# A masked-attention and MLP kernel: additive masks and zero products for the first batch, and a new place in the load order for half a weight

## The chip, the cores and the metric

The kernel runs on one core of a Trainium2 chip. The metric is the device time of one execution in microseconds (us). A quoted time is the median of several executions. A program on one core has no second die to compare with, so an execution is called slow when it lies over 1.5% above the fastest one of the same kernel; ratios use the fast executions alone. The engines are called TensorE (PE in the profile, PEld for its weight loads), VectorE (DVE), ScalarE (ACT), GpSimd (POOL) and SyncE (SP).

## The reference

Attention over 8 batches, 8 heads, 576 positions and 64 columns, followed by a two-layer MLP with the Mish activation over the 8 x 576 = 4608 rows:

```python
rel = pos[:, None] - pos[None, :]
mask_local   = (rel >= 0) & (rel < 32)                                # heads 0 to 3
mask_strided = (rel >= 0) & (pos[None, :] % 32 == pos[:, None] % 32)  # heads 4 to 7
scores = np.where(mask, q @ k.T / sqrt(64), -1e9)
x = (softmax(scores) @ v).transpose(0, 2, 1, 3).reshape(4608, 512)
h = x @ w_in                      # 512 x 2048
out = (h * tanh(softplus(h))) @ w_out   # 2048 x 512
```

Inputs and output are fp32; the kernel computes in bf16 with fp32 sums.

## The kernel before

The MLP goes in nine blocks of 512 rows. Attention of batch 0 runs ahead of it, attention of batch t+1 is woven between the second-layer products of block t. Loads on SyncE's DMA queue bring fp32 that an engine casts; loads on GpSimd's DMA queue cast on the way. From batch 2 on, q and k are turned by DMA transposes, on SyncE's queue too. "Local" tiles end in `l`, strided ones in `s`. These are the parts that the change and the argument touch:

```python
def load_qk_str(b):              # strided k, q: cast on the way, GpSimd's queue
    for dst, src in ((ks, k), (qs, q)):
        nc.gpsimd.dma_start(dst[b % 2][0:PN], src[b, 4:8]...)
def load_qk_loc(b): ...          # local k, q as fp32: SyncE's queue
def load_v(b): load_v_str(b); load_v_loc(b)      # fp32: SyncE's queue
def load_w_in(f0, f1): ...       # GpSimd's queue
def load_w_out(c0, c1): ...      # GpSimd's queue, four pieces in all
def transpose_loc(b):            # kTl, qTl, kTl, qTl: DMA transposes
    for hp in range(2):
        for src, dst in ((kl, kTl[:, hp, 32:]), (ql, qTl[:, hp, :])):
            nc.sync.dma_start_transpose(dst..., src[b % 2]...)
...
def mask(self, kind, i, meng):   # multiply exp(scores) by a mask of 0 and 1
    meng.tensor_tensor(out=pm, in0=pm, in1=mk..., op=ALU.mult)
...
a = Attn(0)
for hp in range(2):              # fp32 strided k, then q: cast, transpose
    cast(Dv, ks[0][0:PN, h:h + 2, :], st0[0][:, h:h + 2, :])
    t_step(0, "s", "k", hp, Sc)
...
for x in (ks, qs):
    Po.memset(x[1][64:SU], 0.0)
Po.tensor_copy(held[:], vs[0][0:1, 3, 0, 0:4])   # GpSimd waits, then loads w_in
load_w_in(0, 256)
... # the other four pieces of w_in, a third of v's cast, local attention
load_qk_str(1)
load_w_out(0, 2)
nc.sync.dma_start(gate[:], w_in[0:1, 0, 1536:1792])  # SyncE waits for w_in
load_v(1)
gT, g1 = mlp1(0, accs)
...
load_qk_loc(2)

def rest_of_w_out():
    Po.tensor_copy(held[:], kTl[0:1, 1, 32:36])      # GpSimd waits for kTl of batch 1
    load_w_out(2, 4)
    load_qk_str(2)
    cast_qk_loc(2, Po, Po)
...
        elif i == 2 and t + 1 < B:                   # block t, third group
            if t + 2 < B:
                load_v(t + 2)
            for b in range(max(3, t + 2 + (t > 1)), min(t + 4, B)):
                load_qk_str(b)                       # t == 1: batches 3 and 4
```

A one-row copy to `held` or a small DMA to `gate` is how the kernel makes an engine's queue wait for data before its next loads.

The softmax here doesn't subtract the row's maximum and nothing guards it: scores larger than these inputs give would overflow.

## Time and profile before

| | before |
|---|---|
| time, three executions | 320.9 us (319.92 to 322.61) |
| span of the profiled one | 319.1 us |
| TensorE busy | 300.1 us, 94% |
| VectorE / ScalarE / GpSimd busy | 127.9 / 172.6 / 41.4 us |
| bytes moved by DMA | 46.72 MB |
| mean granted TensorE clock | 0.999 |

A busy share is an average over the run. Here TensorE is full from the third block on, so what counts is its waits in the first 85 us and what ended each of them. The prediction below shows these views.

### The profile page before, as it was taken

The numbers are of one execution on the slowest core, as the hardware profiler recorded it, in microseconds if no ns is written. First come the engines' busy times: TensorE is split into PE (matmuls) and PEld (weight loads), VectorE is DVE, ScalarE is ACT, GpSimd is POOL, SyncE is SP. The second block draws the span as 40 slices with busy tenths as digits, with TensorE's granted clock in tenths as the row PEclk, the third lists the DMA queues.
The fourth block names the chain that finished last, engine by engine and source line by source line (L and its number), as shares of the span: only waits on it lengthen the run. The fifth ranks groups of instructions, "written<-read, shape, count | busy, mean of one in ns | idle before, by whom it ended". The sixth has DMA issues, their size and how long they took to land.

```text
span 319.1 us, 5867 instructions
## 1 busy us (share of the span) xinstructions
PE 300.1 (94%) x2488; PEld 159.3 (50%) x2488; DVE 127.9 (40%) x332; ACT 172.6 (54%) x195; POOL 41.4 (13%) x50
## 2 busy tenths in 40 slices
PE   0678999999899999999999999999999999999995
PEld 0564455544454445444578555445544554444444
DVE  7672168600577047703870388028802820000000
ACT  2574563476437573767375746664666466315601
POOL 9288030145000100200020000000000000000000
PEclk9999999999999999999999999999999999999999
DMA  6999999999999999999979995898340100011011
GB/s 172 213 235 206 220 212 191 177 221 212 181 184 211 175 192 221 179 153 178 211 160 165 188 208 109 155 191 144 109 83 0 68 32 36 0 66 66 2 59 73
DMA packets 103114, 46.72 MB, mean 146 GB/s; under 512 B 85168, under 2 KB 95728, under 8 KB 103088
## 3 DMA queue, kind: packets, MB, share of 16 engines
q1 hardware_dynamic: 91648, 37.22, 64.6%
q0 software_dynamic: 11152, 8.92, 18.6%
q8 instruction: 19, 0.31, 0.4%
q10 hardware_dynamic: 288, 0.21, 0.2%
q14 instruction: 7, 0.06, 0.1%
HBM read 38.34 MB, written 9.44 MB: 150 GB/s over the span
## 4 chain that ended last, share of the span: by engine, by line
PE 81%; DVE 11%; DMA 4%; ACT 1%; issue 1%; SPq 0%; ACTq 0%
PE psh L428 38%; PE pso L467 28%; PE po L305 4%; PE pso L449 4%; DMA qTl<-ql 3%; PE ps L278 3%; DVE x_l L317 3%; DVE x_s L317 2%; PE trx L344 2%; DVE Pl L289 1%; DVE ks L151 1%; DVE rden L316 1%; DMA st<-in_k_dram 1%; PE trx L354 1%; PE tr L207 1%
## 5 line engine op out<-in xcount | busy, mean ns | idle before, releaser
L428 PE MATMUL psh<-xT,w_in 128*128 128x512 bf16 (+1 forms) x640 | 127.3, 360 | 0.0
L467 PE MATMUL pso<-w_out,gT 128*128 128x512 bf16 x512 | 126.3, 379 | 0.0
L433 ACT ACTIVATE gT<-psh 128x1024 bf16<-128x1024 f32 x72 | 73.6, 1023 | 44.0 <-PE psh L428 43.4
L428 PEld LDWEIGHTS <-w_in 128*128 128x128 bf16 x640 | 62.7, 98 | 62.2 <-issue 1.3
L467 PEld LDWEIGHTS <-gT 128*128 128x128 bf16 x512 | 43.6, 97 | 39.0
L289 DVE TENSOR_TENSOR Ps<-Ps,consts_sb 72x864 bf16<-72x864 bf16 (+1 forms) x24 | 13.2, 551 | 88.8 <-ACT Ps L283 88.8
L149 ACT COPY xT<-trx 128x576 bf16<-128x576 bf16 x32 | 20.1, 639 | 37.7 <-PE trx L354 28.2
L474 ACT COPY osb<-pso 128x1024 f32<-128x1024 f32 x16 | 16.2, 1012 | 22.6 <-PE pso L467 13.8
L283 ACT ACTIVATE Ps<-ps 72x864 bf16<-72x864 f32 (+1 forms) x24 | 18.5, 803 | 14.8 <-PE ps L278 14.8
L316 DVE RECIPROCAL rden<-po 72x4 f32<-72x4 f32 (+1 forms) x100 | 17.4, 174 | 18.8 <-PE po L305 18.6
L317 DVE TENSOR_TENSOR x_s<-po,rden 72x256 bf16<-72x256 f32 x56 | 23.5, 420 | 1.9
L151 DVE COPY osb<-pso 128x512 f32<-128x512 f32 (+1 forms) x2 | 1.1, 558 | 54.5 <-PE pso L449 54.5
L283 ACT ACTIVATE Pl<-ps 128x960 bf16<-128x960 f32 (+1 forms) x24 | 18.7, 806 | 3.6 <-PE ps L278 3.5
L305 PEld LDWEIGHTS <-Ps 72*128 72x128 bf16 x256 | 13.9, 101 | 12.5 <-DVE Ps L289 2.3
L317 DVE TENSOR_TENSOR x_l<-po,rden 96x256 bf16<-96x256 f32 x44 | 18.5, 420 | 1.5
L305 PE MATMUL po<-vs,Ps 72*128 72x65 bf16 x256 | 17.6, 201 | 0.9 <-DVE x_s L331 0.5
L97 POOL DMA_DIRECT2D ks<-in_k_dram x7 | 5.9, 842 | 80.7 <-DMA kTs<-ks 80.7
L305 PE MATMUL po<-vl,Pl 128*128 128x65 bf16 x192 | 12.9, 201 | 2.2 <-DVE x_s L317 0.7
L449 PE MATMUL pso<-w_out,gT 128*128 128x512 bf16 (+1 forms) x80 | 14.0, 336 | 0.0
L305 PEld LDWEIGHTS <-Pl 128*128 128x128 bf16 x192 | 9.9, 103 | 6.4 <-DVE x_l L317 1.8
L289 DVE TENSOR_TENSOR Pl<-Pl,consts_sb 128x960 bf16<-128x960 bf16 (+1 forms) x24 | 13.1, 545 | 0.0
L151 DVE CAST vl<-vl 128x768 bf16<-128x768 f32 x12 | 10.9, 942 | 0.8 <-DMA vl<-in_v_dram 0.8
(70 smaller groups left out, 178.0 us busy)
## 6 DMA issues: line engine op xcount, KB each, us to landing
out_dram<-osb SPq DMA_DIRECT2D x16, 512.0 KB, 3.6
vl<-in_v_dram SPq DMA_DIRECT2D x7, 768.0 KB
vs<-in_v_dram SPq DMA_DIRECT2D x8, 576.0 KB
kl<-in_k_dram SPq DMA_DIRECT2D x7, 576.0 KB, 8.7
ql<-in_q_dram SPq DMA_DIRECT2D x7, 576.0 KB, 9.4
w_out<-in_moe_w_out_dram POOLq DMA_DIRECT2D x4, 512.0 KB, 15.2
ks<-in_k_dram POOLq DMA_DIRECT2D x7, 288.0 KB, 8.0
qs<-in_q_dram POOLq DMA_DIRECT2D x7, 288.0 KB, 9.4
```

Of the source, the lines that this page charges most:

```text
L149: nc.scalar.copy(out_, in_)
L151: eng.tensor_copy(out_, in_)
L283: nc.scalar.activation(pt[0:n, :, 0:nw], ps[0:n, :, o0:o0 + nw], AF.Exp, scale=scale)
L289: meng.tensor_tensor(out=pm, in0=pm, in1=mk[0:n, :].unsqueeze(1).unsqueeze(1).to_broadcast([n, 2, nu, w]), op=ALU.mult,)
L305: nc.tensor.matmul(po[:, h, :], lhsT=pt[0:n, c0:c0 + 128], rhs=rhs, start=True, stop=True,)
L316: nc.vector.reciprocal(rden[0:m, :], po[0:m, :, D])
L317: nc.vector.tensor_tensor(out=dst.rearrange("p (h d) -> p h d", h=4), in0=po[0:m, :, 0:D], in1=rden[0:m, :].unsqueeze(2).to_broadcast([m, ...
L428: nc.tensor.matmul(ps[:, u, o:o + n], lhsT=w_in[:, cc, fc * 128:(fc + 1) * 128], rhs=xT[:, cc, a:a + n], start=(cc == 2), stop=(cc == 1),)
L433: nc.scalar.activation(gT[:, 2 * g:2 * g + 2, :], ps[:], AF.Mish)
L449: nc.tensor.matmul(p, lhsT=gT[:, fc, 128 * ot:128 * ot + 128], rhs=w_out[:, fc, c0:c1], start=(fc == 0), stop=(fc == 15),)
L467: nc.tensor.matmul(p[:, ot % 2, :], lhsT=gT[:, fc, 128 * ot:128 * ot + 128], rhs=w_out[:, fc, :], start=(fc == 0), stop=(fc == 15),)
L474: nc.scalar.copy(osb[:], p[:])
```

## The change

The intent is to begin the MLP earlier and to bring the loads in the order of need. A load whose issue is made to wait for another load's data is called held below; the small DMA that does this on SyncE's queue is the gate. Batch 0's masks become products with a large negative bias that start the score sums; 64 products of zeros keep TensorE busy while it waits; GpSimd's memsets are moved and halved; local v of batch 0 is cast in three pieces on three engines; w_out's second half is issued only when local v of batch 1 has landed; the loads of local q and k of batch 2 come after w_out's third piece; and local v of batch 1 is cast on GpSimd. The first piece of w_in now waits for local q of batch 0 instead of the cast of strided v. The cut leaves out a new layout of local q and k of batch 0 (64 rows of nine positions instead of 96 of six) and a new order of batch 0's products and copies.

```diff
+    zero = const.tile([128, 128], BF16, name="zero")
+    def clear(eng, x):
+        eng.memset(x.bitcast(F32), 0.0)
+    def busy(n, i_acc):
+        ps = acc(i_acc, "ps")
+        for _ in range(n):
+            nc.tensor.matmul(ps[:, 0, 0:128], lhsT=zero[:], rhs=zero[:], start=True, stop=True)
+        def bias(self, kind, i, i_acc):    # ident x bias mask into the score sums
 ...
         a = Attn(0)
+        busy(40, 0)
 ...                                        # 8 + 8 more, and 4 + 4 in xt
+        sb = [a.bias("s", i, i) for i in (1, 2)]
-        a.mask("s", 0, Dv)                 # all six masks of batch 0 go
 ...
-        for x in (ks, qs):
-            Po.memset(x[1][64:SU], 0.0)
-        Po.tensor_copy(held[:], vs[0][0:1, 3, 0, 0:4])
+        Po.tensor_copy(held[P0:P0 + 1], ql0[0:1, 3, 0, 0:4])
         load_w_in(0, 256)
+        for x in (ks, qs):
+            clear(Po, x[1][64:SU].rearrange("p h x -> p (h x)"))
 ...
-        cast_v_loc(0, Po, 0, 3)            # and (0, Sc, 3, 6)
+        cast_v_loc(0, Po, 0, 2)            # and (0, Sc, 2, 4), (0, Dv, 4, 6)
 ...
-        load_qk_loc(2)
         def rest_of_w_out():
-            Po.tensor_copy(held[:], kTl[0:1, 1, 32:36])
+            Po.tensor_copy(held[0:1], vl32[0:1, 3, NW - 1, 0:4])
             load_w_out(2, 4)
             load_qk_str(2)
+            cast_v_loc(1, Po)
+            nc.sync.dma_start(gate[:], w_out[0:1, 8, 0:256])
+            load_qk_loc(2)
             cast_qk_loc(2, Po, Po)
 ...
-                at[6].append(lambda: cast_v_loc(1, Dv, 0, 3))
-                at[7].append(lambda: cast_v_loc(1, Dv, 3, 6))
```

Below, "the front" means all of this but the last two hunks, and "the order" means w_out behind v and q, k of batch 2 behind w_out. The cast of v of batch 1 on GpSimd belongs to neither.

More of the change, by code (lines that the diff above doesn't have):

```diff
@@ L21 @@
 CS, PN = 8, 72
+C0, P0 = 9, 64
 RING = 4
@@ L30, in _consts @@
     p = np.arange(PN)
-    c = np.zeros((128, 128 + WQ + PN), np.float32)
+    c = np.zeros((128, 128 + 2 * WQ + 2 * PN), np.float32)
     c[:, 0:128] = np.eye(128)
     c[:, 128:128 + WQ] = (rel >= 0) & (rel < STRIDE)
-    c[:PN, 128 + WQ:] = (p[:, None] % 4 == p[None, :] % 4) & (p[:, None] <= p[None, :])
+    o = 128 + WQ + PN
+    c[:PN, 128 + WQ:o] = (p[:, None] % 4 == p[None, :] % 4) & (p[:, None] <= p[None, :])
+    c[:, o:o + WQ] = -30000.0 * (1 - c[:, 128:128 + WQ])
+    c[:PN, o + WQ:] = -30000.0 * (1 - c[:PN, 128 + WQ:o])
     return c.astype(ml_dtypes.bfloat16)
@@ L54 @@
     xT = const.tile([128, 4, RT], BF16, name="xT")
-    consts = const.tile([128, 128 + WQ + PN], BF16, name="consts_sb")
+    consts = const.tile([128, 128 + 2 * WQ + 2 * PN], BF16, name="consts_sb")
     ident = consts[:, 0:128]
@@ L58 @@
     stm = consts[0:PN, 128 + WQ:128 + WQ + PN]
+    locb = consts[:, 128 + WQ + PN:128 + 2 * WQ + PN]
+    stmb = consts[0:PN, 128 + 2 * WQ + PN:]
+    zero = const.tile([128, 128], BF16, name="zero")
     vl32 = const.tile([128, 4, NW, D], F32, name="vl32")
@@ L75 @@
     gate = const.tile([1, 256], BF16, name="gate")
-    held = const.tile([1, 4], BF16, name="held")
+    held = const.tile([128, 4], BF16, name="held")
     x_l = const.tile([128, NW, 256], BF16, name="x_l")
@@ L189, in cast_v_loc @@
     def cast_v_loc(b, eng, i0=0, i1=NW):
-        for i in range(i0, i1, 3):
+        n = 3 if i1 - i0 > 2 else 2
+        for i in range(i0, i1, n):
             cast(
-                eng, vl[b % 2][:, i:i + 3, :, 0:D],
-                vl32[:, :, i:i + 3, :].rearrange("p h w d -> p w h d"),
+                eng, vl[b % 2][:, i:i + n, :, 0:D],
+                vl32[:, :, i:i + n, :].rearrange("p h w d -> p w h d"),
             )
@@ L233, in t_step_loc0 @@
         tr = tile_t("tr")[:].bitcast(BF16)
-        for j in range(CL):
+        for j in range(C0):
             for e in range(2):
                 nc.tensor.transpose(
-                    tr[64 * e:64 * e + 64, PL * j:PL * j + PL], src[0:PL, 2 * hp + e, j, :],
-                    ident[0:PL, 0:PL],
+                    tr[64 * e:64 * e + 64, P0 * j:P0 * j + P0], src[:, 2 * hp + e, j, :],
+                    ident[P0:128, P0:128],
                 )
         cast(
-            eng, dst.rearrange("c (p j) -> c p j", j=CL),
-            tr[:, 0:S].rearrange("c (j p) -> c p j", j=CL),
-        )
+            eng, dst.rearrange("c (p j) -> c p j", j=C0),
+            tr[:, 0:S].rearrange("c (j p) -> c p j", j=C0),
+        )
+    def busy(n, i_acc):
+        ps = acc(i_acc, "ps")
+        for _ in range(n):
+            nc.tensor.matmul(ps[:, 0, 0:128], lhsT=zero[:], rhs=zero[:], start=True, stop=True)
     T_ORDER = [(kd, w, hp) for kd in ("s", "l") for hp in range(2) for w in ("k", "q")]
@@ L261, in __init__, with qk @@
             self.b = b
-        def qk(self, parts, i_acc):
-            ps, o = acc(i_acc, "ps"), 0
+        def bias(self, kind, i, i_acc):
+            n, w, mk = (128, WQ, locb) if kind == "l" else (PN, PN, stmb)
+            nu = len(PARTS[kind][i])
+            ps = acc(i_acc, "ps")
+            for e in range(2):
+                nc.tensor.matmul(
+                    ps[:, e, 0:nu * w].rearrange("p (u c) -> p u c", u=nu), lhsT=ident[0:n, :],
+                    rhs=mk.unsqueeze(1).to_broadcast([n, nu, w]), start=True, stop=True,
+                )
+            return ps
+        def qk(self, parts, i_acc, ps=None):
+            first = ps is None
+            if first:
+                ps = acc(i_acc, "ps")
+            o = 0
             todo = []
@@ L277, in qk @@
                             lhsT, rhs = kTs[r, c0:c0 + 128], qTs[r, c0:c0 + PN]
-                        nc.tensor.matmul(ps[:, e, o:o + w], lhsT=lhsT, rhs=rhs, start=True, stop=True)
+                        nc.tensor.matmul(
+                            ps[:, e, o:o + w], lhsT=lhsT, rhs=rhs, start=first, stop=True,
+                            skip_group_check=not first,
+                        )
                     o += w
@@ L334, in pv2, with xt @@
             )
-        def xt(self, kind, hf, eng=None):
+        def xt(self, kind, hf, eng=None, n_busy=0):
             eng = eng or nc.scalar
-            tr = tile_t("trx")[:].bitcast(BF16)
+            tr = tile_t("trx")[:]
+            for _ in range(n_busy):
+                nc.tensor.matmul(tr[:, 320:448], lhsT=zero[:], rhs=zero[:], start=True, stop=True)
+            tr = tr.bitcast(BF16)
             t0 = (self.b % RING) * S
@@ L485 @@
         Po, Dv, Sc = nc.gpsimd, nc.vector, nc.scalar
+        Dv.memset(zero[:], 0.0)
         Sc.preload_act_table(AF.Exp)
@@ L500 @@
         lq0 = g_pool.tile([128, 16, 512], BF16, tag="gT", name="lq0")
-        lq0 = lq0[:].rearrange("p a b -> p (a b)")[0:PL]
-        kl0, ql0 = [lq0[:, 1536 * i:1536 * i + 1536].rearrange("p (h x) -> p h x", h=4) for i in range(2)]
+        lq0 = lq0[:].rearrange("p a b -> p (a b)")[P0:128]
+        kl0, ql0 = [lq0[:, 2304 * i:2304 * i + 2304].rearrange("p (h x) -> p h x", h=4) for i in range(2)]
         for p in P_l:
-            Po.memset(p[:], 0.0)
+            clear(Po, p[:].rearrange("p e c -> p (e c)"))
         for dst, src in ((kl0, k), (ql0, q)):
-            Po.dma_start(dst, src[0, 0:4].rearrange("h (p j) d -> p h (j d)", j=CL))
+            Po.dma_start(dst, src[0, 0:4].rearrange("h (p j) d -> p h (j d)", j=C0))
         kl0, ql0 = [x.rearrange("p h (j d) -> p h j d", d=D) for x in (kl0, ql0)]
@@ L523 @@
             t_step(0, "s", "k", hp, Sc)
+            if hp == 0:
+                busy(8, 0)
+        sb = [a.bias("s", i, i) for i in (1, 2)]
+        busy(8, 0)
+        sb.insert(0, a.bias("s", 0, 0))
         for hp in range(2):
@@ L528 @@
         for i in range(3):
-            a.qk([("s", i)], i)
-        a.mask("s", 0, Dv)
-        cast(Dv, vs[0][0:PN, :, :, 0:D], vs32[0:PN])
-        a.mask("s", 1, Dv)
+            a.qk([("s", i)], i, sb[i])
+        Po.tensor_copy(held[P0:P0 + 1], ql0[0:1, 3, 0, 0:4])
+        load_w_in(0, 256)
         for x in (ks, qs):
-            Po.memset(x[1][64:SU], 0.0)
-        Po.tensor_copy(held[:], vs[0][0:1, 3, 0, 0:4])
-        load_w_in(0, 256)
+            clear(Po, x[1][64:SU].rearrange("p h x -> p (h x)"))
         load_w_in(256, 512)
         load_w_in(512, 1024)
-        cast_v_loc(0, Po, 0, 3)
+        cast_v_loc(0, Po, 0, 2)
         load_w_in(1024, 1536)
@@ L542 @@
         for hp in range(2):
-            t_step_loc0(kl0, kTl[:, hp, 32:32 + S], hp, Sc)
-        a.pv2("s", 0, 0)
-        a.mask("s", 2, Dv)
-        a.pv2("s", 2, 1)
+            t_step_loc0(kl0, kTl[:, hp, 32:32 + S], hp, Sc if hp else Dv)
+        cast(Dv, vs[0][0:PN, :, :, 0:D], vs32[0:PN])
+        lb = [a.bias("l", i, i) for i in range(2)]
         for hp in range(2):
             t_step_loc0(ql0, qTl[:, hp, :], hp, Sc)
-        a.qk([("l", 0)], 2)
-        a.pv2("s", 4, 0)
-        a.qk([("l", 1)], 1)
-        a.mask("l", 0, Dv)
-        a.pv2("s", 6, 0)
-        cast_v_loc(0, Sc, 3, 6)
-        a.qk([("l", 2)], 2)
-        a.mask("l", 1, Dv)
+        a.pv2("s", 0, 2)
+        a.qk([("l", 0)], 0, lb[0])
+        a.qk([("l", 1)], 1, lb[1])
+        a.pv("s", 2)
+        a.pv("s", 3)
+        a.pv2("s", 4, 2)
+        a.qk([("l", 2)], 0, a.bias("l", 2, 0))
+        a.pv("s", 6)
+        a.pv("s", 7)
+        cast_v_loc(0, Sc, 2, 4)
+        cast_v_loc(0, Dv, 4, 6)
+        a.pv2("l", 2, 1)
         load_qk_str(1)
@@ L562 @@
         gT, g1 = mlp1(0, accs)
+        a.pv2("l", 0, 2)
         a.xt("s", 0)
@@ L565 @@
         Sc.preload_act_table(AF.Mish)
-        a.pv2("l", 0, 1)
-        a.mask("l", 2, Dv)
-        a.pv2("l", 2, 0)
-        a.pv("l", 4)
-        a.pv("l", 5)
-        a.xt("l", 0)
-        a.xt("l", 1)
+        a.pv2("l", 4, 0)
+        a.xt("l", 0, n_busy=4)
+        a.xt("l", 1, Dv, n_busy=4)
         cast_qk_loc(1, Po, Po)
         for x in (ks, qs):
-            Po.memset(x[0][64:SU], 0.0)
-        load_qk_loc(2)
+            clear(Po, x[0][64:SU].rearrange("p h x -> p (h x)"))
         def rest_of_w_out():
-            Po.tensor_copy(held[:], kTl[0:1, 1, 32:36])
+            Po.tensor_copy(held[0:1], vl32[0:1, 3, NW - 1, 0:4])
             load_w_out(2, 4)
             load_qk_str(2)
+            cast_v_loc(1, Po)
+            nc.sync.dma_start(gate[:], w_out[0:1, 8, 0:256])
+            load_qk_loc(2)
             cast_qk_loc(2, Po, Po)
@@ L595 @@
                 at[0] = [ts[2], ts[3], cast_v1]
-                at[6].append(lambda: cast_v_loc(1, Dv, 0, 3))
-                at[7].append(lambda: cast_v_loc(1, Dv, 3, 6))
+                at[0].append(lambda: Sc.preload_act_table(AF.Exp))
                 at[9] += [lambda: transpose_str(2), lambda: load_v_loc(2), lambda: cast_v(2, Po, Po)]
```

## The prediction

> **What bounds the kernel now.** I read the page first (busy shares, slices), then the chain that ended last, then TensorE's own waits, then each engine's timeline of the first 60 us, and last the DMA issues, one narrow window at a time so that each issue shows its own landing time. The two rows of the page say where there is anything to win:
>
> ```profile
> PE   0678999999899999999999999999999999999995
> DMA  6999999999999999999979995898340100011011
> ```
>
> A slice is 8 us. TensorE is full except in the first four slices and two thinner ones (at 48 to 56 us and 80 to 88 us, as the waits below show). From the chain, one block in the steady state is 32.5 us (the first product of a block starts at 98.04, the next block's at 130.52), all TensorE, and the change does not touch these blocks. So only the time up to about 85 us can move. The DMA row matters as much: the DMA engines are at 90% or more from 8 us to about 160 us.
>
> TensorE's waits over the whole run (us in total, times, longest):
>
> ```profile
> PE tr L207 <- DVE ks L151: 8.5, 2, 6.9
> PE ps L278 <- DMA qTl<-ql: 1.4, 1, 1.4
> PE trx L344 <- DVE x_l L317: 1.0, 1, 1.0
> PE po L305 <- DVE x_s L317: 0.7, 1, 0.7
> ```
>
> The first is the start of the kernel; the second is at 83.3 to 84.7 us, where attention of batch 2 waits for the last DMA transpose. After it TensorE never waits again for more than the tool reports. The start, VectorE and GpSimd (start us, us):
>
> ```profile
> 4.64 4.46 DVE L151 CAST ks<-st 72x1024 bf16<-72x1024 f32 x2 [0.95 <-DMA st<-in_k_dram]
> 9.03 1.27 DVE L151 CAST qs<-st 72x1024 bf16<-72x1024 f32 x2
> ```
>
> ```profile
> 4.47 1.80 POOL L534 MEMSET ks<- 16x2048 bf16 x1
> 6.21 2.35 POOL L534 MEMSET qs<- 16x2048 bf16 x1
> ```
>
> The same cast takes 2.2 us each on ks and 0.64 us each on qs. The two slow ones lie exactly under the two GpSimd memsets. That is 4.46 - 1.27 = 3.2 us on the way to everything else. From the chain (start us, us):
>
> ```profile
> 0.76 3.86 DMA st<-in_k_dram
> 4.64 4.47 DVE ks L151 x2
> ...
> 26.69 11.33 PE psh L428 x48
> ...
> 75.02 9.65 DMA qTl<-ql
> ...
> 98.04 13.81 PE psh L428 x64
> ```
>
> The MLP starts at 26.5 us. Its first 48 products take 0.236 us each against 0.216 us (13.81/64) later: 48 x 0.020 = about 1.0 us lost to a slow start.
>
> **What the Trainium skill says.** "SBUF — State Buffer", section "Who interferes with whom": VectorE in a two-port mode, which a cast can use, and GpSimd take one port pair by exclusive lock; the one that comes later blocks. The trace agrees: 2.2 us beside a memset, 0.64 us without. "TensorE: Matmul & The Clock Gate", Part 1: the array starts at half clock and is released after some 3.4 us of activity, and falls back after an idle window. The trace agrees in effect: 16 transposes of 72x72 take 1.43 us at 9.76 us and 0.52 us at 42.5 us, though the profile's granted-clock row stays at 9 throughout and doesn't show it. "DMA: Bandwidth & Descriptors", section "Queues, rings and completion order": each DMA engine goes round its queues by packet, so loads on two queues share the engines. The trace agrees: with v of batch 1 on the other queue w_out's second piece took 21.1 us from issue to landing.
>
> **The change part by part.**
> 1. GpSimd's memsets of ks and qs move behind the landing of q of the local heads, and are halved as fp32. The ks casts should take 2 x 0.65 = 1.3 us: -3.2 us on the VectorE chain. But the next thing is the load of q. It's queued ahead of v; a 24 KB piece of v queued behind it and behind the strided v landed at 2.94 + 10.4 = 13.3 us, and the strided v (576 KB) needs some 3.6 us at about 165 GB/s (estimate: 215 to 230 GB/s in the windows, less the casting loads' part), so the second half of q landed at 9 to 9.5 us. GpSimd's first memsets are halved too, so its loads start about 1 us earlier and slow q a little. Before, the qs casts ended at 10.30; I expect 10.0. Of the 3.2 us, about 0.3 us survives here.
> 2. Zero products: 64 of 128x128, in idle time of TensorE. They keep the array warm: transposes and small products on the chain at half their time. From 9.76 to 26.49 TensorE's pieces on the chain sum to about 9 us (0.65 + 0.44 + 1.06 + 0.64 + 0.50 + 0.57 + 0.64 + 0.78 + 0.45 + 1.20 and smaller); I take 2 us off, plus the 1.0 us in the first 48 products.
> 3. Masks of batch 0 by bias products: six VectorE multiplies go (0.60 + 0.60 + 0.44 + 0.64 + 0.64 + 0.35 = 3.3 us), twelve products of 192 to 480 columns come, mostly before the data is there. VectorE also gets a copy of kTl (0.76), one of xT (0.76), a third of v's cast (0.6), and loses bigger evictions to smaller (+0.6). Nearly even for VectorE in sum, but the Exp-multiply-product path loses a hop three times: 1 to 1.5 us.
>    Following the instruction order by hand: Exp of strided scores from 11.4 (before 12.19), local k transposes at 12.5, Exp of local scores 16.1 to 18.5, last evictions to 22.7, MLP from about 23.0. So **3.5 us** at the start of the MLP, and 1.0 us inside it.
> 4. w_in: landing times before were 23.6, 24.4, 27.0, 29.5 and 33.9 us. A start at 23.0 needs them at 23, 23.9, 26.5, 29.9 and 33.4. The first issue comes about 1 us earlier, so this just fits: 0 to 1 us lost.
> 5. Two casts of v (0.94 + 0.94 us, and a memset of 0.27) leave VectorE in block 0 for GpSimd. TensorE's gaps there are 0.69 + 0.25: -0.9 us.
> 6. Second half of w_out after v of batch 1, and the loads of q and k of batch 2 after w_out's third piece. Landing before: w_out 40.7, 44.9, 50.2 and 54.1 us. TensorE used them from 42.85, 47.85, 52.72 and 57.77. There was only 2 to 3.7 us to spare, and now TensorE is 4.5 us earlier.
>
> Sum if data is always there: 3.5 + 1.0 + 0.9 + 1.4 (the wait at 84.7) = 6.8 us at most.
>
> **The rivals.**
> A. *DMA becomes the bound in block 0.* TensorE would want w_out's first piece at 38.5, and it lands at about 40. v of batch 1 starts when w_in has landed (33 us). Sharing with w_out until 44 and then alone, I put its last byte at about 47; then GpSimd issues w_out's third piece (0.75 us, and about a microsecond or more until bytes flow), which lands at about 52 to 53 against a need at 49. Then most of the start's gain is waited away. For it: the DMA row. Against: my bandwidth split is rough.
> B. *The wait at 84.7 us swallows the gain.* The last qTl transpose landed at 84.7 after an unbroken run of issues on the DMA queue since 35.8 us, all of it slowed by full DMA engines. The change removes no bytes, and puts an idle piece of about 2 us (v landed, GpSimd not yet issued) in. So qTl of batch 2 lands between 84 and 87, TensorE waits 3 to 5 us instead of 1.4, and the time is 320 to 322. For it: the later blocks have 3 or more us to spare, this one none. Against: ordering the loads by need may use the queues better, and an earlier TensorE frees buffers earlier.
> C. *Nothing of this binds*: 314.5 to 317 us.
>
> **Range and chances.** I give A and B together a little over half (320 to 321.5), partial relief (317 to 319) a third, C the rest. That makes 319.0 us, with 315.2 to 322.6 for 8 in 10. Faster by over 2% would need all 6.8 us (below 314.5): 4%. Slower by over 2% (above 327.3) would need a new stall of more than 6 us: 2%.
>
> **What would show it.** Right: ks casts of about 0.65 us; MLP start near 23 us and its first 48 products at 0.216 us; no multiply of Ps and Pl in batch 0; the gaps at 55 to 57.6 us gone; TensorE waiting for DMA of w_out at 38 to 53 us, or of qTl near 85 us, where it resumes no earlier than 84. Wrong: qTl landing 3 us or more earlier than before, or w_in keeping the MLP back to 25 us, or slow casts coming back because the moved memsets meet other VectorE casts.

## The result, and the profile after

The changed kernel took 330.99 us (328.74 to 332.12, four executions) against 321.75 us for the kernel before in the same rounds. The ratio is 1.0284, with a 95% interval of 1.0207 to 1.0361. A ratio here is the mean time of one kernel's fast runs over that of the other's of the same rounds, so it isn't quite the ratio of the two medians. The profiled spans are 327.0 and 319.1 us, and the mean granted clock fell from 0.999 to 0.968. The prediction's range (315.2 to 322.6) did not hold it.

The rows of the page after, in slices of 8.2 us (TensorE, granted clock, DMA):

```profile
PE   7789986999389999999999999999999999999996
PEclk9759999999879999999999999999999999999999
DMA  7999968999999999999979899696750101011012
```

TensorE is busier in the first four slices, where the zero products count as busy. Two holes have opened: at 41 to 57 us in the DMA row (6 and 8), with a 6 for TensorE beside it, and a 3 for TensorE at 82 to 90 us. The clock row is no longer flat; "half clock" below means a granted clock of 0.50.

VectorE and GpSimd at the start, after (start us, us):

```profile
4.96 0.69 DVE L161 CAST ks<-st 72x1024 bf16<-72x1024 f32 x1 [1.20 <-DMA st<-in_k_dram]
6.32 0.69 DVE L161 CAST ks<-st 72x1024 bf16<-72x1024 f32 x1 [0.66 <-DMA st<-in_k_dram]
7.72 0.69 DVE L161 CAST qs<-st 72x1024 bf16<-72x1024 f32 x1 [0.72 <-DMA st<-in_q_dram]
9.86 0.69 DVE L161 CAST qs<-st 72x1024 bf16<-72x1024 f32 x1 [1.44 <-DMA st<-in_q_dram]
...
15.54 0.94 POOL L155 MEMSET ks<- 16x1024 f32 x1
```

The slow casts are gone, with the memsets now at 15.5 us. But the last cast ends at 10.55 us, where it ended at 10.30 before: the piece of q that it waits for lands later.

The chain of work that ended last, after (start us, us, what):

```profile
3.69 16.36 DMA vl<-in_v_dram
21.19 1.21 POOL w_in L143
22.39 12.37 DMA w_in<-in_moe_w_in_dram
36.22 12.56 DMA vl<-in_v_dram
49.09 5.75 DMA w_out<-in_moe_w_out_dram
54.87 1.02 PE pso L505 x4
...
81.67 9.46 DMA qTl<-ql
...
105.91 7.77 PE psh L466 x36
```

Before, this chain went through the slow casts and TensorE. Now it is loads from 3.7 to 54.8 us, each waiting for the one ahead: v of batch 0 holds GpSimd's cast, this holds the issue of w_in's last pieces, these hold SyncE's gate ahead of v of batch 1, and v holds w_out's third piece. The first product of block 2, at 98.04 us before, is at 105.91 us: +7.87 us, all of the difference of the spans (7.9).

TensorE's waits after (us in total, times, longest):

```profile
PE ps L310 <- DMA qTl<-ql: 6.7, 1, 6.7
PE pso L505 <- DMA w_out<-in_moe_w_out_dram: 3.1, 1, 3.1
PE tr L218 <- DVE qs L161: 1.2, 1, 1.2
```

The 8.5 us on the casts of ks have become about 1.9 us (0.7 on ks, 1.2 on qs), partly because zero products fill the time. The wait for the last transpose grew from 1.4 to 6.7 us, and one for w_out is new.

Where the DMA engines pause shows in the table of stretches. Its columns are the stretch, then busy time and count of TensorE, weight loads, VectorE, ScalarE and GpSimd, then granted clock, DMA share and GB/s. Before:

```profile
44.00:46.00 2.00, 2.00 (x32) 1.04 (x29) 1.82 (x3) 1.24 (x2) 0.53 (x1) 1.00 1.20 225
46.00:48.00 2.00, 1.99 (x24) 0.99 (x23) 0.74 (x2) 1.39 (x2) 0.00 (x0) 1.00 1.27 211
48.00:50.00 2.00, 2.00 (x25) 1.09 (x23) 1.52 (x5) 0.63 (x2) 0.00 (x0) 1.00 1.20 194
50.00:52.00 2.00, 2.00 (x26) 1.14 (x25) 1.24 (x5) 0.56 (x3) 0.00 (x0) 1.00 1.21 195
```

And after, with the stretch behind the second wait:

```profile
44.00:46.00 2.00, 1.93 (x31) 1.02 (x31) 1.56 (x2) 0.96 (x2) 0.00 (x0) 1.00 0.89 163
46.00:48.00 2.00, 2.00 (x26) 1.11 (x26) 0.84 (x4) 0.81 (x1) 0.00 (x0) 1.00 0.21 44
48.00:50.00 2.00, 1.84 (x23) 1.05 (x19) 1.60 (x5) 1.02 (x2) 1.17 (x3) 1.00 0.00 1
50.00:52.00 2.00, 1.78 (x24) 1.00 (x22) 1.61 (x5) 0.97 (x1) 2.00 (x3) 1.00 0.66 62
...
88.00:90.00 2.00, 0.00 (x0) 0.00 (x0) 0.00 (x0) 0.00 (x0) 0.00 (x0) 0.50 1.34 174
90.00:92.00 2.00, 0.83 (x16) 0.69 (x17) 0.00 (x0) 0.54 (x1) 0.00 (x0) 0.50 1.25 189
92.00:94.00 2.00, 1.78 (x11) 0.90 (x10) 0.60 (x2) 1.34 (x3) 0.00 (x0) 0.50 1.36 188
```

From 46 to 52 us the engines move (44 + 1 + 62) x 2 us = 214 KB; at the 163 to 225 GB/s around it this is about 1 us of work, so some 5 us are lost (an estimate). In stretches of half a microsecond the pause has two parts: from 46.5 to 48.5 us the last bytes of v come in alone, at 24, 18, 16 and 3 GB/s; from 48.5 to 50.5 us nothing moves, while GpSimd sees v (48.83), issues w_out (49.09) and its first bytes are on their way. And TensorE comes out of its long wait at half clock until about 94 us, which costs over 1 us more.

What SyncE's queue issues then, before and after (the local q, k loads of batch 2 and the last transpose):

```profile
35.82 9.70 SPq L109 DMA_DIRECT2D kl<-in_k_dram  x1
75.02 1.63 SPq L180 DMA_TRANSPOSE qTl<-ql  x1
```

```profile
54.85 0.51 SPq L624 DMA_DIRECT2D gate<-w_out  x1
55.45 0.53 SPq L116 DMA_DIRECT2D kl<-in_k_dram  x1
81.67 1.75 SPq L190 DMA_TRANSPOSE qTl<-ql  x1
```

The load of k of batch 2 is issued 19.6 us later and the last transpose 6.65 us later. Most of the 19.6 us is made up for, because SyncE issues the same list in 26.2 us (55.45 to 81.67) instead of 39.2 us (35.82 to 75.02): the issue of k alone took 9.70 us before and 0.53 us after. The transpose then takes 9.46 us to land, as it took 9.65 before.

### The profile page after: what moved, and what is told of

It reads as the page before. It is cut to its first block, busy times and chain, and to the rows that moved or that the text cites. A ratio compares the mean times of both kernels' runs of the same rounds, so it can differ in the third digit from the quotient of the medians.

```text
span 327.0 us, 6038 instructions
## 1 busy us (share of the span) xinstructions
PE 305.1 (93%) x2548; PEld 165.7 (51%) x2588; DVE 122.9 (38%) x329; ACT 171.3 (52%) x193; POOL 37.3 (11%) x53
## 3 DMA queue, kind: packets, MB, share of 16 engines
q0 software_dynamic: 10896, 8.92, 18.1%
## 4 chain that ended last, share of the span: by engine, by line
PE 72%; DMA 17%; DVE 6%; issue 1%; SPq 1%; POOL 1%; ACT 0%; POOLq 0%; ACTq 0%
PE psh L466 34%; PE pso L505 26%; DMA vl<-in_v_dram 9%; PE pso L487 4%; DMA w_in<-in_moe_w_in_dram 4%; PE po L340 3%; DMA qTl<-ql 3%; PE ps L310 3%; DVE x_l L352 2%; DMA w_out<-in_moe_w_out_dram 2%; DVE x_s L352 2%; DVE rden L351 1%; PE trx L382 1%; DVE Pl L324 1%; PE trx L392 1%
## 5 line engine op out<-in xcount | busy, mean ns | idle before, releaser
L505 PE MATMUL pso<-w_out,gT 128*128 128x512 bf16 x485 | 122.5, 381 | 5.5 <-DMA w_out<-in_moe_w_out_dram 3.1
L466 PE MATMUL psh<-xT,w_in 128*128 128x512 bf16 (+1 forms) x628 | 125.7, 358 | 0.8 <-issue 0.2
L324 DVE TENSOR_TENSOR Ps<-Ps,consts_sb 72x864 bf16<-72x864 bf16 (+1 forms) x21 | 12.2, 581 | 87.8 <-ACT Ps L318 87.8
L159 ACT COPY xT<-trx 128x576 bf16<-128x576 bf16 x31 | 19.6, 639 | 36.2 <-PE trx L392 28.5
L318 ACT ACTIVATE Ps<-ps 72x864 bf16<-72x864 f32 (+1 forms) x24 | 18.5, 803 | 21.8 <-PE ps L310 21.8
L352 DVE TENSOR_TENSOR x_s<-po,rden 72x256 bf16<-72x256 f32 x60 | 25.2, 421 | 2.1
L352 DVE TENSOR_TENSOR x_l<-po,rden 96x256 bf16<-96x256 f32 x42 | 17.7, 421 | 1.4
L310 PE MATMUL ps<-qTl,kTl 64*128 64x96 bf16 x192 | 8.2, 216 | 7.1 <-DMA qTl<-ql 6.7
L104 POOL DMA_DIRECT2D ks<-in_k_dram x7 | 5.2, 741 | 80.1 <-DMA kTs<-ks 80.1
L324 DVE TENSOR_TENSOR Pl<-Pl,consts_sb 128x960 bf16<-128x960 bf16 (+1 forms) x21 | 11.5, 545 | 0.0
```

The costliest lines, as they stand in the source:

```text
L159: nc.scalar.copy(out_, in_)
L310: nc.tensor.matmul(ps[:, e, o:o + w], lhsT=lhsT, rhs=rhs, start=first, stop=True, skip_group_check=not first,)
L318: nc.scalar.activation(pt[0:n, :, 0:nw], ps[0:n, :, o0:o0 + nw], AF.Exp, scale=scale)
L324: meng.tensor_tensor(out=pm, in0=pm, in1=mk[0:n, :].unsqueeze(1).unsqueeze(1).to_broadcast([n, 2, nu, w]), op=ALU.mult,)
L352: nc.vector.tensor_tensor(out=dst.rearrange("p (h d) -> p h d", h=4), in0=po[0:m, :, 0:D], in1=rden[0:m, :].unsqueeze(2).to_broadcast([m, ...
L466: nc.tensor.matmul(ps[:, u, o:o + n], lhsT=w_in[:, cc, fc * 128:(fc + 1) * 128], rhs=xT[:, cc, a:a + n], start=(cc == 2), stop=(cc == 1),)
```

## The experiments

The first theory was: the order costs the time, by the pause of the DMA engines and the late q and k of batch 2. Its rivals: the zero products hurt (clock, or room on TensorE), or the front itself does. Seventeen kernels ran. All gave correct results. Ratios are to the kernel before; the kernel before had medians of 321.65 to 322.44 us. Kernels are compared only within the same rounds. Profiled times named below are of single executions.

**1. The order undone, in the changed kernel** (v of batch 1 is still cast on GpSimd).

```diff
+        load_qk_loc(2)
         def rest_of_w_out():
-            Po.tensor_copy(held[0:1], vl32[0:1, 3, NW - 1, 0:4])
+            Po.tensor_copy(held[0:1], kTl[0:1, 1, 32:36])
             ...
-            nc.sync.dma_start(gate[:], w_out[0:1, 8, 0:256])
-            load_qk_loc(2)
```

> The changed kernel with the order of loads alone as before: w_out's second half is held on kTl, and q and k of batch 2 are loaded without a gate. Theory G (the two gates leave the DMA engines idle near 46 to 51 us, and everything on the queue behind that lands late): no slice near 46 to 51 us under 150 GB/s, the last qTl of batch 2 lands at 84 to 86 us instead of 91, TensorE's wait for it falls from 6.7 to 2 to 5 us, time 318 to 321.5 us. Rival Z (zero products upset the granted clock and that costs the time): 328 us or more, as changed. Rival D (the DMA engines are simply full, whatever the order): qTl still lands near 91 us.

Measured: 325.73 us, 1.0095 (1.0018 to 1.0171). Two thirds of the loss go, but it does not come out faster than before. The pause is gone (no stretch of 2 us from 42 to 52 us is under 186 GB/s), and so is the wait for the transpose. A wait of 6.5 us on v of batch 1 has appeared.

**2. The order alone, in the kernel before** (the same hunks the other way round).

> The kernel before with the new order of loads alone (no zero products, no bias masks, casts of v where they were). G: a stretch of 4 us or more under 100 GB/s after 43 us, qTl lands 5 to 7 us later than 84.7, time 326 to 329 us. Z: 320 to 322 us. D: 320 to 323 us.

Measured: 328.61 us, 1.0202 (1.0143 to 1.0262). In the profile the DMA engines pause again (6 GB/s from 46 to 48 us, 31 from 48 to 50), the last transpose is issued at 79.60 us, and TensorE waits for it:

```profile
PE ps L278 <- DMA qTl<-ql: 6.0, 1, 6.0
```

So the order alone makes most of the loss, without a zero product or a bias in the kernel.

**3. No zero products, in the changed kernel** (`range(n)` and `range(n_busy)` become `range(0)`). The expectation says 72 products; there are 64 (40 + 8 + 8 and twice 4).

> The changed kernel without the 72 zero products. G: the wait for qTl decides, so 329 to 332 us as changed, with the MLP start 0 to 1.5 us later and the wait shorter by as much. Z: the granted clock stays at 1.00 in 12 to 26 us and the time falls to 323 us or less.

Measured: 331.51 us, 1.0279 (1.0216 to 1.0343), the same as with them.

```profile
PE ps L310 <- DMA qTl<-ql: 8.5, 1, 8.5
PE tr L218 <- DVE ks L161: 6.5, 2, 5.7
PE pso L505 <- DMA w_out<-in_moe_w_out_dram: 1.1, 1, 1.1
```

The first 48 MLP products take 12.69 us instead of 10.49, so the zero products are worth 2.2 us there. The waits for w_out and the transpose change from 3.1 + 6.7 to 1.1 + 8.5 us, and nothing is gained or lost in the end. The zero products fall as a cause. The MLP begins no later without them (25.23 us, against 25.6), and the cast of local v of batch 0 on GpSimd starts at 19.08 us.

**4. The loads of q and k of batch 2 not held back; w_out still behind v.**

```diff
+        load_qk_loc(2)
         ...
-            nc.sync.dma_start(gate[:], w_out[0:1, 8, 0:256])
-            load_qk_loc(2)
```

> The changed kernel with q and k of batch 2 loaded without the gate, w_out's second half still behind v. G: these loads fill the idle stretch, qTl lands at 84 to 87 us, time 319 to 323 us, though w_out's third piece may come later than 54.8 us. If the late w_out is what costs (3.1 us wait, then the rest follows): 328 us or more.

Measured: 326.5 us, 1.0128 (1.0067 to 1.019). The wait on the transpose is gone and w_out, which now shares the engines, is waited for instead:

```profile
PE pso L505 <- DMA w_out<-in_moe_w_out_dram: 7.6, 2, 7.3
```

So without the hold on q and k about 1.6 points of the 2.8 go, and what is left is paid at another wait.

**5. The hold halved** (one word: GpSimd waits for strided v, `vs32`, which lands before local v, `vl32`).

> The changed kernel with one edit: w_out's second half is held on the strided v, both gates else as changed. Theory G: w_out is issued near 44.5 instead of 49.1 us, the idle stretch goes, w_out's third piece lands 3 to 4 us earlier (51 to 52), the gate opens as much earlier, the last qTl lands at 87 to 88.5, time 326.5 to 328.5. Rival D (DMA engines simply full): qTl lands near 91 as before, 330 or more.

Measured: 326.4 us, 1.0124 (1.0068 to 1.0181). The pause shrinks (141 GB/s from 44 to 46 us, 93 from 46 to 48), w_out's third piece lands at 50.4 us instead of 54.8, and the last transpose at 88.55 instead of 91.13 us. TensorE, earlier by then, still waits 7.6 us for it. So the length of the pause counts, and the transpose stays the bound.

**6. The hold halved and q, k not held back** (experiments 4 and 5 together).

> The changed kernel with w_out's second half held on the strided v (lands near 44 us) and not on the local v (48.8), and q and k of batch 2 ungated. Theory G: no stretch under 150 GB/s between 40 and 60 us, w_out's third piece lands at 51 to 54 us, local v at 50 to 54 us, TensorE's waits in block 0 sum to 2 to 5 us, none over 2 us for qTl, time 319 to 323. Theory V (v cannot finish while w_out is being loaded): local v lands near 57 us or later, time 323 to 327.

Measured: 326.16 us, 1.0121 (1.0073 to 1.017); waits of 2.2 us on w_out and 4.1 us on the transpose. The two gains do not add.

**7. As 6, with all five pieces of w_in issued ahead of GpSimd's memsets and cast.**

> The same as the run before with GpSimd's five issues of w_in put ahead of its two memsets and its cast of v. If GpSimd's place in the queue is what made w_in land at 34.8 us (0.9 later than before, after a wait for v at 20 us): w_in lands at 32.5 to 33.9, v of batch 1 starts 1 to 2 us earlier, and the time is 1 to 2 us below the run before. If the DMA engines are the limit there: w_in lands within 0.5 us of 34.8 and the time is the same.

Measured: 325.91 us, 1.0113 (1.0065 to 1.016), the same time as 6. By the gate, w_in lands at 33.99 us, 0.8 us earlier than in the changed kernel but only 0.3 us earlier than in 6 (34.31), so the edit moved its date little. The wait for w_out goes, the one on the transpose is 4.6 us, and the MLP begins later, at 26.92 us. A miss for the idea that GpSimd's order alone holds w_in's date and the total.

**8. The front alone** (the order as before, and v of batch 1 cast on VectorE as before).

> The first 43 us of the change alone: order of loads as before and v of batch 1 cast on VectorE as before. In the run with only the order undone, v of the local heads landed at 59 us and TensorE waited 6.5 us for its cast on GpSimd. Theory V (v itself lands late, because it starts 1 us later and shares the DMA engines with w_out all the time): VectorE now waits for v until 57 to 60 us, TensorE waits about 5 to 7 us, time 323 to 326. Rival P (the cast on GpSimd, in order behind other work, is what was late): v is there by 53 us as before, time 316 to 319.

Measured: 324.86 us, 1.0058 (1.0012 to 1.0104); 323.6 to 328.28 us. So the front does not gain even by itself. Its loss and that of the order (0.58% and 2.02%) nearly add up to the whole (2.84%), but nothing shows that they are its parts: the late v that costs here isn't in the changed kernel, where v landed at 48.78 us. The profile, of the slowest of the six, shows why it can lose, first in TensorE's waits, then in the table of stretches:

```profile
PE po L340 <- DVE x_s L352: 7.3, 2, 6.3
```

```profile
56.00:58.00 2.00, 0.00 (x0) 0.00 (x0) 0.00 (x0) 0.00 (x0) 0.00 (x0) 0.93 1.13 139
58.00:60.00 2.00, 0.00 (x0) 0.00 (x0) 0.13 (x1) 0.00 (x0) 0.00 (x0) 0.50 0.27 34
60.00:62.00 2.00, 0.25 (x4) 0.24 (x4) 1.85 (x5) 0.00 (x0) 0.00 (x0) 0.50 0.97 198
```

VectorE is named as the releaser, but it was itself waiting for local v of batch 1, issued at 37.15 us and landed at 59.85 us, 22.7 us later. In the kernel before it was there by 52.7 us. The same happened in experiment 1 (59.1 us).

**9. The front with the old dates of the loads** (GpSimd's first memsets at their old length, w_in released by the cast of strided v as before).

> The front of the change (bias masks, zero products, third piece of v's cast) with every load's start as in the kernel before: GpSimd's first memsets at their old length, w_in held on the cast of v and issued in the old order, the memsets of ks and qs after w_in; order of loads and casts in block 0 as before. Theory L (the front's earlier start of the local q, k and of w_in takes bandwidth from v of batch 0, which landed at 20.1 instead of 18.1 us, and so from all that is chained behind): v of batch 0 lands by 18.5, the MLP starts at 23 to 25 us, w_in lands by 34 us, v of batch 1 by 54 us, time 317.5 to 321. Rival S (the array's falling back to half clock and the longer instruction path hold the start): MLP start no earlier than 25.4 and time 322 or more.

Measured: 326.64 us, 1.0142 (1.0108 to 1.0177); v of batch 1 still lands late, at 58.5 us, and the MLP begins at 25.93 us, as rival S said. A miss for theory L, but not a clean test: v of batch 0 landed only at about 19.8 us, and not every load had its old date (strided k of batch 1 was issued at 24.56 us instead of 20.72, w_out's first piece at 26.02 instead of 22.17).

**10. and 11. Strided q and k of batch 4 moved one block later in the program text**, in the kernel before and on top of 9.

```diff
-                    for b in range(max(3, t + 2 + (t > 1)), min(t + 4, B)):
+                    for b in ([3] if t == 1 else [4, 5] if t == 2 else range(t + 3, min(t + 4, B))):
```

> The kernel before with one edit: the strided q and k of batch 4 are loaded a block later, so that two of the four GpSimd loads issued at 74 to 77 us no longer run beside the last DMA transposes of batch 2. If these loads are what stretched the last qTl to 9.65 us (against 4.8 for the one before it): it lands 2 to 4 us earlier, TensorE's wait of 1.4 us for it goes, time 319.5 to 321 against 321.7. If not: the same landing, the same time.

> Both edits together, the candidate for the best version. Under L and with the loads moved: no wait for qTl over 1 us, time 316 to 319.5. Under S: 321 or more.

Measured: 321.99 us, 0.9995 (0.9961 to 1.003), and 327.54 us, 1.016 (1.0118 to 1.0201). Both say nothing of their question. Nothing on GpSimd's queue held these loads, so all four were issued between 75.3 and 78.5 us, beside the transposes as before: a place in the program is not a time. They stand as a control and as a repeat of 9.

A second theory was made from all traces so far. The distance from the issue of local v of batch 1 to the issue of w_out's second half was 6.3 us before, 8.2 in 10, 8.6 to 13.6 in the variants with v in time, but 4.4, 3.7, 5.0 and 4.85 us in 1, 8, 9 and 11, where v was late. The front makes w_in land later, so v is issued later, and kTl is ready earlier, so w_out is issued earlier.

**12. That distance cut in the kernel before.**

```diff
-            Po.tensor_copy(held[:], kTl[0:1, 1, 32:36])
+            Po.tensor_copy(held[:], kTl[0:1, 0, 32:36])
```

> The kernel before, with one edit: the second half of w_out is released by the first head pair of kTl (copied at 38.3 to 39.1 us) instead of the second, so that it is issued near 39.3 us instead of 41.6, only about 4 us behind v of batch 1 (35.3). Theory gap (v of batch 1 lands late whenever w_out's second half is issued less than about 5 us behind it): v lands at 57 to 59 us, TensorE waits about 5 us more in the first block, time 325 to 327 us. Rival (the late landing of v comes of other parts of the new front, such as the casting queue's different order): v lands by 53 us as in before and the time is 321 to 322.5 us.

Measured: 321.11, 325.19, 326.57 and 326.56 us. The ratio of the fast runs is 1.003 (0.9963 to 1.0098), but it counts only two of the four. The profile fell on the first: w_out issued at 40.46 us, 4.4 us behind v (36.03), v in time, a wait of 0.5 us for the transpose, clock 1.00. That distance is as short as in 1, 9 and 11, where v was late, so the distance alone does not decide. The others ran at clocks of 0.995 and 0.989, where the kernel before had 1.00 in nearly all executions, and all three lie within the time that the theory expects; two of these count as slow. But the kernel before, too, had one execution of 328.03 us at a clock of 0.99, and no trace of a late execution was taken, so the experiment is inconclusive.

**13. That distance widened, with the front alone** (8).

```diff
-            Po.tensor_copy(held[0:1], kTl[0:1, 1, 32:36])
+            Po.tensor_copy(held[0:1], qTs[0:1, 8 * SU:8 * SU + 4])
...
-                at[0] = [ts[2], ts[3], cast_v1]
+                at[0] = [ts[2], ts[3], cast_v1, rest_of_w_out]
...
-                    if i == 8:
-                        rest_of_w_out()
```

> The new front with the load order of before, where w_out's second half is called later and released by the copy of qTs instead of kTl, so that it is issued near 44.5 us, some 8 us behind v of batch 1. Theory gap: v lands by 53 us, no long wait in block 0, time 318.5 to 321 us. Rival (the front itself costs): 324 to 326 us as without the edit.

Measured: 324.32 us, 1.0087 (1.0041 to 1.0133). w_out is issued at 45.68 us, 8.9 us behind v (36.8), and v is there when VectorE casts it at 53.1 us; the 6.3 us wait is gone. The edit delays strided q and k of batch 2 and GpSimd's casts along with w_out, so it does not show that the distance to w_out alone is the cure. And the time did not follow (the profile is of one of the two longest executions, 327.79 us):

```profile
PE ps L310 <- DMA qTl<-ql: 5.3, 1, 5.3
PE pso L505 <- DMA w_out<-in_moe_w_out_dram: 1.7, 1, 1.7
```

TensorE now comes to the last transpose of batch 2 early and waits there, and half clock follows (0.50 from 88 to 94 us).

**14. Strided q and k of batches 3 and 4 really held, in the kernel before.**

```diff
+                    if t == 1:
+                        Po.tensor_copy(held[:], qTl[0:1, 1, 0:4])
                     for b in range(max(3, t + 2 + (t > 1)), min(t + 4, B)):
                         load_qk_str(b)
```

> The kernel before, with a one-row copy on GpSimd of the last head pair of qTl ahead of the loads of strided q and k of batches 3 and 4, so that these loads, which an earlier run failed to move, really start only after the last transpose of batch 2's local q has landed. Theory (these loads stretch that transpose from about 5 us to 10): it lands 2 to 4 us earlier, the 1.4 us wait of TensorE on it goes, time 320 to 321 us. Rival (the transpose is long for other reasons): no change of its landing, time 321 to 322.5.

Measured: 320.22 us, 0.994 (0.9913 to 0.9968). The loads start at 78.3 us instead of 74.0. The transpose, issued at 74.37 us, has landed when GpSimd's copy of it runs at 77.77 us: 3.4 us instead of 9.65. TensorE goes through without a wait (its timeline):

```profile
83.64 0.46 PE L278 MATMUL ps<-qTl,kTl 64*128 64x96 bf16 x14
```

So these loads had made the transpose long. Block 2 begins at 96.85 us instead of 98.04.

**15. Experiments 13 and 14 together, on the front.**

> Both of the last two edits on the new front: if both theories hold, 316 to 319.5 us, faster than the kernel before. If only the gap theory holds, 318.5 to 321. If neither holds, 324 to 327.

Measured: 321.75 us, 0.9981 (0.994 to 1.0023). The long waits of blocks 0 and 1 are gone (0.7 us for w_out is left), and block 2 begins at 95.43 us, 1.4 us ahead of experiment 14. In block 2, though, batch 3's strided loads, issued 3 us later than in 14, come too late for their transposes (issued from 99.66 instead of 96.87 us):

```profile
115.54 0.22 PE L310 MATMUL ps<-qTl,kTl 64*128 64x96 bf16 x2 [0.66 <-DMA qTl<-ql]
116.71 0.43 PE L310 MATMUL ps<-qTl,kTl 64*128 64x96 bf16 x12 [0.95 <-DMA qTl<-ql]
```

and in the table of stretches:

```profile
118.00:120.00 2.00, 2.00 (x10) 0.83 (x8) 1.27 (x5) 0.85 (x1) 0.00 (x0) 0.51 1.40 172
```

The two waits are 1.6 us, and half clock from 118 to 121 us follows. The next block starts at 131.54 us, against 129.33 in 14.

**16. and 17. Only batch 4 held; and both batches held on the last kTl transpose instead, one issue earlier.**

```diff
-                    if t == 1:
-                        Po.tensor_copy(held[0:1], qTl[0:1, 1, 0:4])
                     for b in range(...):
+                        if b == 4:
+                            Po.tensor_copy(held[0:1], qTl[0:1, 1, 0:4])
                         load_qk_str(b)
```

> The combined kernel (new front, order of before, w_out's second half later, strided q and k held on the last transpose), with batch 3's strided loads let go again and only batch 4's held. In the combined kernel the held loads of batch 3 made its transposes start at 99.7 us instead of 96.9 us and TensorE waited 0.7 + 1.0 us in block 2, with half clock after. Theory (that wait comes of batch 3's late loads, and batch 4's loads alone had stretched the last transpose of batch 2): neither wait, 317.5 to 320 us. Rival (batch 3's own loads stretch the transpose of batch 2): the wait of block 1 returns by 2 to 5 us and the time is 321 to 324 us.

Measured: 322.92 us, 1.0013 (0.9962 to 1.0064). The rival holds. Batch 3's loads alone, issued at 77.25 us, stretch the transpose (issued at 78.03 us, landed by GpSimd's copy):

```profile
86.28 0.18 POOL L667 COPY held<-qTl 1x4 bf16<-1x4 bf16 x1 [7.62 <-DMA qTl<-ql]
```

That is 8.2 us, and TensorE waits 3.4 us for it.

> The combined kernel with both batches' loads held on the last kTl transpose instead of the last qTl transpose, which was issued 1.3 us later. Theory (batch 3's loads start some 1.3 us earlier, enough to take most of the 1.7 us wait in block 2, while only the last 2 us of the transpose share the queue with them): 318.5 to 321 us. Rival (even a small overlap stretches that transpose): a wait of 1 us or more on qTl in block 1 and no gain over the combined kernel's 321.75 us.

Measured: 317.53 to 325.11 us, median 322.33; three of the six count as slow, and the fast three give 0.9929 (0.9861 to 0.9997). The profile fell on a slow one: no wait in block 1, 4.1 + 0.8 us in block 2. This version scatters too widely to be called a gain.

**The best version** is experiment 14: one copy of four elements added to the kernel before. At 320.22 us it is 0.6% faster than the kernel before, by an interval that leaves out 1, and it beats the changed kernel. No version with the new front was reliably faster than the kernel before.

## Why the prediction was wrong

The time is 8.4 us above the top of the range. Taking the steps in the prediction's own order:

1. *Step 1, casts of ks.* Right: 0.69 us each for "about 0.65". Of the 3.2 us, "about 0.3 us survives here" was too hopeful: the casts of qs ended at 10.55, not 10.0 us.
2. *Step 2, zero products.* Half right. The first MLP products took 10.49 us (47 of the 48 are recorded), against 12.69 for 48 without them. Up to 12 us the small products were faster too: eight transposes took 0.43 us, 0.66 before. But from about 13 to 26 us the granted clock is 0.50 in the changed kernel, though TensorE is recorded as busy for all of 12 to 16 us. Two figures of the prediction are off: the pieces it adds up on the chain make 6.9 us, not about 9, and 16 transposes at 42.3 us took 0.69 us (42.33 to 43.02), not 0.52, so the early ones took twice as long.
3. *Step 3 and the start.* "MLP from about 23.0" failed. By the records it began at 25.6 us (the first record seems to be missing), 0.9 us earlier than before, not 3.5. ScalarE was late on the way there (start us, us):

```profile
17.43 1.92 ACT L318 ACTIVATE Pl<-ps 128x960 bf16<-128x960 f32 x2 [0.65 <-POOL qs L155]
19.97 0.49 ACT L318 ACTIVATE Pl<-ps 128x384 bf16<-128x384 f32 x1 [0.62 <-PE ps L310]
20.36 0.61 ACT L159 CAST vl<-vl 128x512 bf16<-128x512 f32 x1
```

(The releaser that the first line names is doubtful; in experiment 3 the same wait ends with TensorE's scores.) The Exp of the local scores ran from 17.4 to 20.5 us instead of 16.1 to 18.5, ScalarE's cast of v followed without a gap, TensorE waited 0.6 us for that cast, and ScalarE's last copy of xT ended at 25.7 us, where the prediction had 22.7. Local v of batch 0 had landed at 20.05 us (about 18.1 before), just ahead of that cast, and in experiment 3 it was there by 19.1 us with the MLP at 25.2. So the path of instructions held the start, part of it at half clock, and not the date of v; how much of the delay is half clock is not shown.

4. *Step 4, w_in.* The prediction let the last piece land by about 33.4 us, ahead of the old 33.9, as the first issue came earlier. It landed at 34.76 us: its issue stood on GpSimd behind the cast of local v of batch 0, which came 2 us later than before. The loads of local q and k and of w_in had moved about 1 us forward; that they slowed this v is inferred. The MLP did not wait for it, but v of batch 1 did, and was issued 0.9 us later.
5. *Step 5, casts off VectorE.* Right: the gaps of 0.69 and 0.25 us shrank to one of 0.24 us, at 58.8 us.
6. *Rival A.* Right in kind: v landed at 48.78 us for 47, w_out's third piece at 54.84 for 52 to 53, and TensorE waited 3.1 us. That used up the gain: TensorE came to the last transpose of batch 2 at 84.48 us, 1.15 us later than before, so even on its old date of landing (84.67) that transpose would have left nothing gained.
7. *Rival B* names the mechanism that decided, and **its size is the step that failed**: "puts an idle piece of about 2 us (v landed, GpSimd not yet issued) in. So qTl of batch 2 lands between 84 and 87". The pause was some 5 us. The piece that the prediction named, from v's landing (48.78 us) to w_out's first bytes (about 50.5), was 1.7 us of it; it left out that v's own last bytes would come in slowly with nothing else to load. And qTl landed at 91.13 us, so TensorE waited 6.7 us, not 3 to 5. The landing is 6.46 us later; the other 1.41 us of the 7.87 us at block 2 is about what half clock from 91.1 to 94 us costs (half of 2.9 us, an estimate). The prediction says that the clock falls back after an idle window, but puts no cost on it behind this wait.

"A new stall of more than 6 us: 2%" was therefore far too little. The prediction saw the loss of the early gain as the worst case, and gave next to no chance to a *hold* that delays the transposes by more than some 2 us. Experiments 2, 4 and 5 show the hold as a cause: the order alone loses 2.0%, without the hold on q and k over half of the loss goes (2.8 to 1.3%), and with a shorter pause as much (1.2%). Experiment 3 clears the zero products.

What the prediction did not see at all is that the front, by itself, moves v of batch 1 and w_out's second half towards each other. Experiment 8 shows the late v, and in 13, with a distance of 8.9 us (and strided q and k of batch 2 delayed along with w_out), v is in time. Where the front's gain goes is shown by 13 and 15: for each wait taken away, another opens at a later date that a DMA sets.

Still open: why v comes so late in the new front when w_out is issued within about 5 us, and whether the distance is the cause at all: in the kernel before, experiment 12's profile had v in time at 4.4 us. No view shows single DMA engines' order. Open also is why the new front scatters by up to 2% between executions (experiments 8, 13 and 17), and how much of 15's result would be left with its block 2 mended.

## What to carry to other kernels

A hold that brings loads in the order of need waits for the very last byte of a load, then for an issue and the next first bytes. Here that left full DMA engines with some 5 us of little or nothing to do, and the last transpose of the queue came 6.65 us later. Work out the new landing date of the next *critical* load before you count compute. An earlier start is worth only the slack of the next date that a load sets; follow the chain of dates to the first block that has slack. And look for the one transfer that lands just in time and ask which loads run beside it, since holding those back was the only gain here.

## What the Trainium skill lacked or had wrong

- "TensorE: Matmul & The Clock Gate", Part 1, ties half clock in its table to an idle window of some 3.4 us (a later passage tells of frequent short idle times too, without a length). The runs agree for long waits (0.50 after 6.7 us in the changed kernel), but show it after less: in experiment 15, with waits of 0.66 and 0.95 us, TensorE was busy for 2.39 of the 4 us from 114 to 118 us, and the clock was 0.51 from 118 to 120 us; in the changed kernel TensorE was busy for 1.41 of the 3 us from 9 to 12 us, and the clock was 0.50 by 13 us. It was still 0.50 at 16 us, with TensorE recorded as busy from 12 to 16 us on 91 short products (whose ends are modelled). The page warns in general that clock events in a trace are unreliable; the case here is half clock missed at the start: in the kernel before the row shows 9 throughout, yet 8 small transposes at the start took 0.66 us that take 0.42 us later.
- "DMA: Bandwidth & Descriptors", section "DMA Transpose (X-bar)", gives no duration, and the page nowhere says what other loads do to it (elsewhere it has only an effective bandwidth). Here the last transpose of batch 2 took 3.4 us with the engines otherwise left to its queue's own loads (14), 8.2 us beside one batch's casting loads (16), and 9.65 us beside two batches' (the kernel before).
- The same page's "Queues, rings and completion order" describes the turns between queues by packet. It does not say how late the end of a load can come: local v of batch 1 took 22.7 us in experiment 8 and 12.56 us in the changed kernel, for the same 768 KB, and in the latter its last bytes came at 3 to 24 GB/s for 2 us with nothing beside them.
